# Who adds up the six modulation rows: a TensorE product per row, or VectorE and GpSimd sums with TensorE adding over partitions

## The chip, the cores and the metric

The kernel runs on one NeuronCore of a Trainium2 chip. The metric is the device time of one execution in microseconds (us). For the kernel before, three runs were timed: 2280.32, 2281.99 and 2283.0 us, median 2281.99. A hardware profile of one further execution lies beside them: that execution took 2280.29 us, and its span, from the first to the last instruction, is 2278.5 us. So 1.8 us lie outside the span, and the profiled execution stands at the lower end of the runs, 1.7 us under their median.

In what follows PE is the TensorE matmul unit and PEld its weight load, DVE is VectorE, ACT is ScalarE, POOL is GpSimd, and SP is the engine whose queue issues all DMAs here. An entry such as L244 is a line of the kernel.

## What is computed

A transformer block on 2048 tokens of width 576, in float32: 32 query heads of 18 channels share one key and value head, and the second half is an MLP of width 4608. Both halves are modulated. One vector `c` of 576 numbers goes through a silu and a 576 x 3456 matrix, and the result is cut into six rows of 576: shift, scale and gate for either half.

```
mod = (silu(c) @ w_mod).reshape(1, 6, 1, 576)
sa, ca, ga, sb, cb, gb = mod[:, 0], ..., mod[:, 5]
h = layernorm(x) * (1 + ca) + sa
x = x + ga * attention(h, wq, wk, wv, wo)
h = layernorm(x) * (1 + cb) + sb
x = x + gb * (gelu(layernorm(h) @ w1 + b1) @ w2 + b2)
```

Rows 0 and 1 are needed at once, before the first projection. Rows 3 and 4 (`sb`, `cb`), 2 (`ga`, folded into `wo`) and 5 (`gb`, folded into `w2` and `b2`) are needed later.

## The kernel before

The work on each engine stands in an order written out by hand; every engine runs its own instructions strictly in that order, and waits where an operand or a buffer is not ready. All DMAs share SP's queue, so an issue that waits holds up the ones behind it.

**Opening (about 0 to 33 us).** The first 512 tokens are loaded, normalised and transposed (`tr`, L152) into five PSUM tiles `hp`. Meanwhile rows 0 and 1 are made: for each row its five chunks of 128 rows of `w_mod` (`wm01`, tile `bigw`) are multiplied on PE with the silu of `c`, in two halves of 288 columns. `mod_mm` (L199) does that: `srep` holds each value of silu(c) 32 times over, so the five products of a half go to four strips of 32 partitions, and the strips hold partial sums. DVE copies them to `modr` (L201). `mod_cols` (L207) then turns a row into columns: a matmul with `sel`, a matrix with ones in partitions 0, 32, 64 and 96, adds the four strips. The result `mcol` is scale and bias of `h_evac` (L224), where ACT makes `hf` from `hp`, DVE casts it to the high half of `zt` (L226) and subtracts for the low half (L229). In between ACT and POOL split the projection weight `wqr` into `wqh` and `wql` (L379, L381), first the last 128 columns, then the first 504; DVE does the last 64 rows (L385).

**Projection (to 137 us).** The four token blocks `tb` are projected one after the other, five pieces (`q_chunk`, 14 matmuls of L244 each) a block. Of the first piece of a block, `k_block` (L287) makes keys as soon as the second piece has been issued; it reads the low half `qs[:,1]` that POOL made at L276. In the last block four `mod_bcast` steps are strewn between the pieces: rows 3 and 4 go through `mod_mm`, then `sel` as stationary matrix adds the strips and lays the sum on all 128 partitions at once (L217), and DVE stores it to `BC` (L218).

**Attention (137 to about 1402 us).** 32 quads of four heads. A quad takes 64 score matmuls (L855), each followed by an exponential on ACT (L857), the products with V (L845), and the row maxima of the next quad (L315 on PE, L877 on DVE). Scores and all odd jobs share the four PSUM buffers `psB`. The token strings `QUAD` and `QUADW` are that order. After each chunk `kc` of 16 the function `between` may advance two generators: `fill`, every second chunk, and `prep` (the MLP weights, on POOL), from quad 3 on. At the head of `fill` stands `late_weights`: rows 2 and 5 by `mod_bcast`, and then `wo` times row 2, on POOL (L511 to L513). In `between` a new query tile is cleared too (`new_q`, POOL, L132), which waits until PE is done with the quad three before. After a quad `post_quad` divides: DVE transposes and takes a reciprocal (L675, L678), POOL multiplies (L679), DVE transposes back (L681).

**MLP (to the end).** Nothing of the change lies there.

Of the kernel before, what the change touches and what calls it, by code (L numbers as in the profile page):

```python
# [18 lines left out]
KD = 5  # L19
# [13 lines left out]
def block_kernel(ctx: ExitStack, tc, x, wqkv, wo, w1, b1, w2, b2, c, wmod, ident_in, out):  # L33
# [52 lines left out]
    srep = pa.tile([128, KD, 32], F32, name="srep")  # L86
# [14 lines left out]
    for h2 in range(2):  # L101
        sy.dma_start(wm01[1][:, :, 288 * h2:288 * (h2 + 1)], wmod[1, :, :, 288 * h2:288 * (h2 + 1)])
# [9 lines left out]
    sel = pa.tile([128, 128], F32, name="sel")  # L112
# [3 lines left out]
    st = p1.tile([128, KD], F32, name="st")  # L116
# [74 lines left out]
    modr = p1.tile([128, 2, D], F32, name="modr")  # L191
    mcol = p1.tile([128, 2, KD], F32, name="mcol")

    def mod_mm(wm, h2, dst):

        pm = psB()
        for k in (0, 4, 1, 2, 3):
            g = 32 * (k % 4)
            pe.matmul(pm[g:g + 32, :288], srep[:, k, :], wm[:, k, 288 * h2:288 * (h2 + 1)],  # L199
                      start=(k < 4), stop=(k > 0))  # L200
        ve.tensor_copy(dst[:, 288 * h2:288 * (h2 + 1)], pm[:, :288])  # L201

    def mod_cols(j, pm):
        for m in range(KD):
            w = 128 if m < KD - 1 else 64
            for o in ((0,) if m < KD - 1 else (0, 64)):
                pe.matmul(pm[o:o + w, m:m + 1], modr[:, j, 128 * m:128 * m + w], sel[:, :1], start=True, stop=True)  # L207
        ve.tensor_scalar(mcol[:, j, :], pm[:, :KD], float(j), None, op0=ALU.add)

    def mod_bcast(wm, row, dst, add, scl):  # L210

        for h2 in range(2):
            mod_mm(wm, h2, row)
            yield
            cs = slice(288 * h2, 288 * (h2 + 1))
            p = psB()
            pe.matmul(p[:, :288], sel, row[:, cs], start=True, stop=True)  # L217
            ve.tensor_scalar(dst[:, cs], p[:, :288], scl, add, op0=ALU.mult, op1=ALU.add)  # L218
            yield

    def h_evac(p, zt, k, e, first=False):

        hf = p1.tile([128, TB], F32, name="hf", bufs=2)
# [153 lines left out]
    def split_wq(cs, es):  # L377
        for k in range(KD):
            ac.activation(wqh[:, k, cs], wqr[:, k, cs], AF.Copy)  # L379
        for k in range(KD - 1):  # L380
            es[k].tensor_tensor(wql[:, k, cs], wqr[:, k, cs], wqh[:, k, cs].bitcast(F32), op=ALU.subtract)  # L381
# [4 lines left out]

    pick = p1.tile([128, 2, 128], F32R, name="pick")
    ones = p1.tile([128, 1], F32, name="ones")
    ve.memset(pick.bitcast(F32), 0.0)
    for i, r in ((0, 0), (0, 2), (1, 1)):  # L390
        ve.tensor_copy(pick[:, i, :].rearrange("p (g c) -> p g c", g=2)[:, :, DH * r:DH * (r + 1)],
                       ident[:, None, 96:96 + DH].to_broadcast([128, 2, DH]))
    ve.tensor_reduce(ones, ident.rearrange("p (g c) -> p g c", g=2)[:, :, R3:], axis=AX.XY, op=ALU.add)
# [27 lines left out]
    split_rest(slice(0, 504))  # L421

# [17 lines left out]
    wm34 = []  # L440
    late = (x for j in range(2) for x in mod_bcast(wm34[j], modr[:, j], BC[:, j, :], float(j), 1.0))
    for tb in range(NB):
        nz = big() if tb + 1 < NB else None
        if tb >= 2:
            wm34.append(load_mod(tb + 1))
        for i, m in enumerate((4, 0, 1, 2, 3)):
# [14 lines left out]
            if tb == NB - 1:  # L461
# [4 lines left out]
                for _ in range((0, 1, 2, 2, 2)[i]):  # L466
# [883 lines left out]
```

## Time and profile before

| | |
|---|---|
| median of 3 runs | 2281.99 us |
| the profiled execution | 2280.29 us |
| its span | 2278.5 us |
| PE busy | 2241.0 us, 98% of the span |
| DVE busy | 1942.0 us, 85% |
| ACT busy | 1644.9 us, 72% |
| POOL busy | 1506.1 us, 66% |
| opening: first matmul for the keys of block 0 | at 33.31 us |
| first score matmul of quad 0 | at 137.00 us |
| quad 0, quad 1, quads 2 and 3 | 42.2, 41.0, 37.4 us each |

The quads are counted from the first exponential of one to the first of the next. A busy PE is not PE at its peak, since matmuls overlap and their ends are modelled; so a stage is read from when its pieces start, and from what a wait ended on, rather than from the busy shares.

### The profile page before, as it was taken

Reading aid. Unit: us, or ns where it says so; the run is one execution under the profiler, and the core shown is the slowest. Engines: PE = TensorE matmul, PEld = TensorE weight load, DVE = VectorE, ACT = ScalarE, POOL = GpSimd, SP = SyncE. Lnnn points to the kernel's source line nnn. Section 1 sums busy time; section 2 is a strip of 40 time slices with the busy share of each in tenths; the row PEclk is TensorE's granted clock in tenths of the full one; section 3 lists DMA queues with packets and bytes.
Section 4 is the critical chain, followed back from the end, with each engine's and each line's share of the span. In section 5 each row is a group of like instructions: output and inputs, shape, how many; then the busy total and the mean of one; then the engine's idle time right before and its main releaser. Section 6 shows DMA issues by size and latency. Waiting matters only on the chain.

```text
span 2278.5 us, 45948 instructions
## 1 busy us (share of the span) xinstructions
PE 2241.0 (98%) x16534; PEld 1446.2 (63%) x16534; DVE 1942.0 (85%) x3435; ACT 1644.9 (72%) x3141; POOL 1506.1 (66%) x1759
## 2 busy tenths in 40 slices
PE   8999999999999999999999999999999999999999
PEld 6644545444444444444444546888888878888888
DVE  6589999999999999999999974778888777787786
ACT  5558999999999999999999997444454444343443
POOL 6503366676787787677783002888888887767676
PEclk9999999999999999999999999999999999999999
DMA  6421234433433333333331002555656557666563
GB/s 225 138 99 49 73 124 142 136 128 117 135 124 121 119 132 114 119 125 123 119 129 64 20 7 83 180 174 178 177 173 180 160 151 215 180 178 179 177 181 117
DMA packets 184229, 305.58 MB, mean 134 GB/s; under 512 B 19275, under 2 KB 77515, under 8 KB 184001
## 3 DMA queue, kind: packets, MB, share of 16 engines
q1 hardware_dynamic: 184001, 302.64, 42.1%
q8 instruction: 131, 2.15, 0.4%
q14 instruction: 97, 0.79, 0.1%
HBM read 200.48 MB, written 93.19 MB: 129 GB/s over the span
## 4 chain that ended last, share of the span: by engine, by line
PE 90%; DVE 5%; POOL 2%; ACT 2%; issue 1%; DMA 0%; ACTq 0%; POOLq 0%; DVEq 0%
PE psC L845 22%; PE psB L1053 17%; PE psA L1150 16%; PE psB L855 14%; PE psM L315 11%; PE psB L657 2%; PE psB L244 2%; DVE mx L877 2%; PE psB L865 2%; PE psB L152 1%; ACT P L857 1%; PE psA L315 1%; PE psB L199 1%; PE psA L1180 1%; PE psA L657 1%
## 5 line engine op out<-in xcount | busy, mean ns | idle before, releaser
L857 ACT ACTIVATE P<-psB 128x512 f32<-128x512 f32 x2008 | 1044.8, 619 | 45.3 <-PE psM L315 18.4
L877 DVE TENSOR_REDUCE mx<-psM 128x1 f32<-128x512 f32 x1476 | 938.1, 683 | 42.4 <-PE psB L855 19.6
L315 PE MATMUL psM<-KS,qst 64*128 64x512 f32 x1722 | 600.1, 440 | 1.1 <-DVE mx L877 0.4
L855 PE MATMUL psB<-qst,KS 64*128 64x512 f32 x2008 | 584.5, 428 | 0.6 <-DVE mx L333 0.4
L845 PE MATMUL psC<-P,V 128*32 128x256 f32 (+3 forms) x6424 | 578.8, 448 | 0.5 <-ACT O L672 0.5
L855 PEld LDWEIGHTS psB<-qst,KS 64*128 64x128 f32 x2008 | 302.2, 184 | 215.6 <-ACT P L857 132.8
L1053 PE MATMUL psB<-ops,w1a 128*128 128x512 f32 x1512 | 395.7, 397 | 0.2 <-DVE h L1068 0.2
L315 PEld LDWEIGHTS psM<-KS,qst 64*128 64x128 f32 x1722 | 274.5, 184 | 157.2 <-DVE mx L877 122.4
L1053 PEld LDWEIGHTS psB<-ops,w1a 128*128 128x128 f32 x1512 | 271.4, 189 | 45.9 <-DVE h L1068 0.4
L1156 DVE TENSOR_TENSOR XT<-psA,XT 128x576 f32<-128x576 f32 x350 | 256.4, 753 | 18.5 <-PE psA L1150 11.5
L845 PEld LDWEIGHTS psC<-P,V 128*32 128x32 f32 x6424 | 139.4, 108 | 202.9 <-issue 176.7
L1150 PE MATMUL psA<-w2s,big 128*128 128x288 f32 x1680 | 248.3, 297 | 6.4 <-POOL big L1123 2.6
L1150 PEld LDWEIGHTS psA<-w2s,big 128*128 128x128 f32 x1680 | 240.0, 190 | 21.7 <-POOL big L1123 3.5
L1124 POOL TENSOR_TENSOR big<-s,big 128x512 fp32r<-128x512 f32 x140 | 181.9, 1299 | 11.2
L1066 ACT ACTIVATE psB<-gs 128x512 f32<-128x512 f32 x144 | 86.7, 602 | 135.5 <-DVE gs L1065 135.5
L1062 ACT ACTIVATE h<-psB,b1t 128x512 f32<-128x512 f32 x144 | 98.0, 680 | 109.1 <-PE psB L1053 93.7
L875 DVE CUSTOM_DVE_ANT_0 xc<-psM,xc 128x512 f32<-128x512 f32 x246 | 166.0, 681 | 3.7 <-PE psB L855 1.2
L868 ACT ACTIVATE xc<-psB 128x512 f32<-128x512 f32 x246 | 152.9, 622 | 11.9 <-PE psM L315 11.9
L691 POOL TENSOR_TENSOR os<-O,os 128x512 fp32r<-128x512 f32 x28 | 36.1, 1290 | 150.5 <-ACT os L690 150.5
L1065 DVE SCALAR_TENSOR_TENSOR gs<-psB,h 128x512 f32<-128x512 f32 x144 | 98.5, 684 | 39.3 <-ACT psB L1063 39.3
L718 POOL TENSOR_TENSOR r<-r,r 128x256 fp32r<-128x256 f32 (+1 forms) x162 | 121.4, 749 | 13.0
L132 POOL MEMSET qst<- 32x1024 f32 x62 | 58.6, 945 | 106.8 <-PE psB L855 69.0
(198 smaller groups left out, 3238.9 us busy)
## 6 DMA issues: line engine op xcount, KB each, us to landing
w1a<-w1scr SPq DMA_DIRECT2D x252, 256.0 KB
w2s<-w2sum SPq DMA_DIRECT2D x140, 288.0 KB
w1scr<-r SPq DMA_DIRECT2D x126, 256.0 KB
w2scr<-r SPq DMA_DIRECT2D x72, 288.0 KB
w2sum<-r SPq DMA_DIRECT2D x72, 288.0 KB
w2s<-w2scr SPq DMA_DIRECT2D x70, 288.0 KB
qst<-qscr SPq DMA_DIRECT2D x192, 72.0 KB
w1a<-w2scr SPq DMA_DIRECT2D x35, 288.0 KB
```

Source lines behind the costliest of these rows:

```text
L315: pe.matmul(o, QST[n][64 * g:64 * g + 64, p, 128 * qt:128 * (qt + 1)], KS[64 * g:64 * g + 64, 512 * kb:512 * (kb + 1)], start=True, stop=True)
L718: po.tensor_tensor(o[:, n:2 * n], src, o[:, :n].bitcast(F32), op=ALU.subtract)
L845: pe.matmul(PVt[n][32 * j:32 * (j + 1), cs], V[:, kc, :], t[:, j, cs], start=(kc == 0 and h0 == 0), stop=(kc == 15), skip_group_check=True)
L855: pe.matmul(t, KS[64 * g:64 * g + 64, 128 * kc:128 * (kc + 1)], QST[n][64 * g:64 * g + 64, i, :], start=True, stop=True)
L857: ac.activation(P[n, kc][:, 2 * i + g, :], t, AF.Exp, scale=SCALE)
L868: ac.activation(XC[-1], t, AF.Relu)
L875: ve.tensor_tensor_reduce(c, t, c, 1.0, -3.0e38, ALU.add, ALU.max, o)
L877: ve.tensor_reduce(o, t, axis=AX.X, op=ALU.max)
L1053: pe.matmul(o, x, y, start=(first and i == 0), stop=(i == len(terms) - 1), skip_group_check=True)
L1124: po.tensor_tensor(unit(u, 1), x, unit(u, 0).bitcast(F32), op=ALU.subtract)
L1150: pe.matmul(p[:, i, :288], x[:, ts_], W2S[k][:, y], start=(bool(first) and q == 0), stop=(q == 2), skip_group_check=True)
L1156: ve.tensor_tensor(o, p[:, :, :288], o, op=ALU.add)
```

## The change

- **Row 1** is no longer made by PE. Its load comes in three pieces by chunks (two, two, one) instead of two by columns. DVE multiplies chunk 0 with the per-partition value of silu(c) and adds the other four by `scalar_tensor_tensor` (`mod_sum`); every partition then holds a partial sum, and `mod_cols` adds over all 128 with a column of `unity`, a matrix of ones.
- **Row 0** stays on PE; of the fifth chunk each strip now takes 72 columns, 4 + 4 matmuls a half instead of 5.
- **The weight split** is given chunk by chunk; the last three chunks of 504 columns go behind `h_evac` on ACT, the last two on POOL. The low halves of `zt` of chunks 1 and 3 go from DVE to POOL, `hf` has three buffers instead of two, and `pick` and `ones` are made later.
- **Rows 2 to 5** are made in the first quads. All of 5, 2 and 3 are loaded when `fill` starts, 4 later. POOL multiplies each with silu(c) and adds the chunks in place (`scaled`, `added`: six instructions a row, 2880 elements a partition multiplied and 2304 added). `bcast` then needs two matmuls with `unity` for a row, one for each half, back to back, and two DVE stores. Nothing of it is left in the projection.
- `prep` begins in quad 4 instead of 3; in `ln2_rows` a step lies between loading and scaling `b2`; the buffer of the first attention output is taken in `late_weights`.

```
-    for h2 in range(2):
-        sy.dma_start(wm01[1][:, :, 288 * h2:288 * (h2 + 1)], wmod[1, :, :, 288 * h2:288 * (h2 + 1)])
+    for k0, k1 in ((0, 2), (2, 4), (4, 5)):
+        sy.dma_start(wm01[1][:, k0:k1], wmod[1, :, k0:k1])
...
-    def mod_mm(wm, h2, dst):
+    def mod_mm(h2):
         pm = psB()
-        for k in (0, 4, 1, 2, 3):
-            g = 32 * (k % 4)
-            pe.matmul(pm[g:g + 32, :288], srep[:, k, :], wm[:, k, 288 * h2:288 * (h2 + 1)],
-                      start=(k < 4), stop=(k > 0))
-        ve.tensor_copy(dst[:, 288 * h2:288 * (h2 + 1)], pm[:, :288])
+        c0 = 288 * h2
+        for k in range(KD - 1):
+            pe.matmul(pm[32 * k:32 * k + 32, :288], srep[:, k, :], wm01[0][:, k, c0:c0 + 288], start=True, stop=False,
+                      skip_group_check=True)
+        for k in range(KD - 1):
+            pe.matmul(pm[32 * k:32 * k + 32, 72 * k:72 * k + 72], srep[:, KD - 1, :],
+                      wm01[0][:, KD - 1, c0 + 72 * k:c0 + 72 * k + 72], start=False, stop=True, skip_group_check=True)
+        ve.tensor_copy(modr[:, 0, c0:c0 + 288], pm[:, :288])
+    def mod_sum(k):
+        row, w, c = modr[:, 1], wm01[1][:, k, :], st[:, k:k + 1]
+        if k:
+            ve.scalar_tensor_tensor(row, w, c, row, op0=ALU.mult, op1=ALU.add)
+        else:
+            ve.tensor_scalar(row, w, c, None, op0=ALU.mult)
...
-        hf = p1.tile([128, TB], F32, name="hf", bufs=2)
+        hf = p1.tile([128, TB], F32, name="hf", bufs=3)
...
-            mod_mm(wm01[0], t, modr[:, 0])
-    mod_mm(wm01[1], 0, modr[:, 1])
-    mod_cols(0, psB())
-    mod_mm(wm01[1], 1, modr[:, 1])
-    busy(2)
-    mod_cols(1, psB())
+            for k in (0, 1) if t == 0 else (2,):
+                mod_sum(k)
+            mod_mm(t)
+    for k in (3, 4):
+        mod_sum(k)
+    mod_cols(0, psB(), sel)
+    mod_cols(1, psB(), unity[:, :1])
     busy(5)
-    split_wq(slice(504, WQC), (po, po, po, po))
-    split_wq(slice(0, 504), (po, po, po, po))
     for k in range(KD):
-        h_evac(hp[k], zt, k, ve, True)
+        split_wq(k, slice(504, WQC))
+    for k in range(2):
+        split_wq(k, slice(0, 504))
+    for k in range(KD):
+        h_evac(hp[k], zt, k, po if k % 2 else ve, True)
         if k == 0:
             split_rest(slice(504, WQC))
+    for k in range(2, KD):
+        split_wq(k, slice(0, 504))
     split_rest(slice(0, 504))
...
-        if tb >= 2:
-            wm34.append(load_mod(tb + 1))
...
-                for _ in range((0, 1, 2, 2, 2)[i]):
-                    next(late)
...
     def late_weights():
...
+        def scaled(w, k0, k1):
+            po.tensor_tensor(w[:, k0:k1], w[:, k0:k1], st[:, k0:k1, None].to_broadcast([128, k1 - k0, D]), op=ALU.mult)
+        def added(w, k0, k1, n=1):
+            po.tensor_tensor(w[:, k0:k0 + n], w[:, k0:k0 + n], w[:, k1:k1 + n], op=ALU.add)
...
+        def bcast(w, dst, add, scl):
+            for h2 in range(2):
+                cs = slice(288 * h2, 288 * (h2 + 1))
+                p = psB()
+                pe.matmul(p[:, :288], unity, w[:, 0, cs], start=True, stop=True)
+                ve.tensor_scalar(dst[:, cs], p[:, :288], scl, add, op0=ALU.mult, op1=ALU.add)
+            yield
+        m3, m2, m5 = (bigw(D) for _ in range(3))
+        for j, t in ((5, m5), (2, m2), (3, m3)):
+            sy.dma_start(t, wmod[j])
...
+        for i in range(12):
+            for _ in range(2):
+                next(sums, None)
+            if i > 5 and i % 2:
+                next(rows)
+            yield
+        m4 = load_mod(4)
...
-        if n > 2 and kc not in quiet:
+        if n > 3 and kc not in quiet:
```

Three places show how instructions move. First PE in the last block of the projection, before, from the keys of the block (L287) to the first score matmul (L855); `bigw` is a modulation row, `modr` its partial sums, `mxf` the maxima of quad 0:

```order
L287 MATMUL psB<-qs,pick 128x512 x2
L293 MATMUL psB<-ident,qf 128x128 x4
L199 MATMUL psB<-bigw,srep 32x288 x5
L244 MATMUL psB<-big,wA 126x512 x7
L315 MATMUL psA<-KS,qst 128x512 x4
L244 MATMUL psB<-big,wA 126x512 x7
L217 MATMUL psB<-modr,sel 128x288
L199 MATMUL psB<-bigw,srep 32x288 x5
L244 MATMUL psB<-big,wA 126x512 x5
L315 MATMUL psA<-KS,qst 128x512 x4
L244 MATMUL psB<-big,wA 126x512 x5
```

And the same stretch after (L290 was L287, L247 was L244, L318 was L315):

```order
L290 MATMUL psB<-qs,pick 128x512 x2
L296 MATMUL psB<-ident,qf 128x128 x4
L247 MATMUL psB<-big,wA 126x512 x7
L318 MATMUL psA<-KS,qst 128x512 x4
L247 MATMUL psB<-big,wA 126x512 x12
L318 MATMUL psA<-KS,qst 128x512 x4
L247 MATMUL psB<-big,wA 126x512 x5
```

The `mod_mm` (L199) and `sel` (L217) steps are gone, here and twice more up to the first score matmul; the rest follows on unchanged.

Second, POOL in the opening after the change, from the first weight split (L383, before L381) to the low half of the first projected piece (L279, before L276):

```order
L383 TENSOR_TENSOR wA<-bigw,wA 128x128 x4
L383 TENSOR_TENSOR wA<-bigw,wA 128x504 x2
L232 TENSOR_TENSOR big<-hf,big 128x512 x2
L383 TENSOR_TENSOR wA<-bigw,wA 128x504 x2
L279 TENSOR_TENSOR qs<-qf,qs 128x512
```

Before, the eight splits stood together; now two subtractions for `zt`, which wait for DVE's casts, stand among them.

Third, DVE in the same stretch after the change, from the sums of row 1 (L215, L213) to the last chunk of `zt`; L207 stores halves of row 0, L222 the columns:

```order
L215 TENSOR_SCALAR modr<-bigw,st 128x576
L213 SCALAR_TENSOR_TENSOR modr<-bigw,st,modr 128x576
L207 COPY modr<-psB 128x288
L213 SCALAR_TENSOR_TENSOR modr<-bigw,st,modr 128x576
L207 COPY modr<-psB 128x288
L213 SCALAR_TENSOR_TENSOR modr<-bigw,st,modr 128x576 x2
L222 TENSOR_SCALAR mcol<-psB 128x5 x2
L229 CAST big<-hf 128x512
L232 TENSOR_TENSOR big<-hf,big 128x512
L387 TENSOR_TENSOR wA<-bigw,wA 64x128
L229 CAST big<-hf 128x512 x2
L232 TENSOR_TENSOR big<-hf,big 128x512
```

DVE gains the five sums, loses two copies, and of the five subtractions for `zt` (one behind each cast before) keeps those of chunks 0, 2 and 4.

More of the change, by code (lines that the diff above doesn't have):

```diff
@@ L111, in block_kernel @@
     ve.memset(nhalf, -0.5)
-    sel = pa.tile([128, 128], F32, name="sel")
+    unity = pa.tile([128, 128], F32, name="unity")
+    po.memset(unity, 1.0)
+    sel = p1.tile([128, 1], F32, name="sel")
+    srep = p1.tile([128, KD, 32], F32, name="srep")
     ve.memset(sel, 0.0)
@@ L385, in split_rest @@
         ve.tensor_tensor(o, wqr[64:, KD - 1, cs], o.bitcast(F32), op=ALU.subtract)
[L387 to L393, printed above, removed]
     def busy(n):
```

66 lines of the change are left out of this document (38 added, 28 removed).

## The prediction

> **What bounds the kernel now.** I read the page's totals and the chain first, then one row per stage, then the waits inside the stages that the change touches.
>
> ```profile
> span 2278.5 us, 45948 instructions
> ...
> PE 90%; DVE 5%; POOL 2%; ACT 2%; issue 1%; DMA 0%; ACTq 0%; POOLq 0%; DVEq 0%
> ```
>
> Nine tenths of the chain that ended last are PE. So the question for every edit is whether it takes a step out of PE's order, or a wait that PE sits in. The attention quads by stretches (columns: stretch, length, then busy time and count of PE, PEld, DVE, ACT, POOL, granted clock, DMA share, GB/s); each stretch runs from a quad's first exponential to the next one's:
>
> ```profile
> 137.60:179.80 42.20, 41.33 (x357) 20.07 (x356) 37.78 (x73) 36.63 (x73) 0.40 (x1) 0.96 0.23 81
> 179.80:220.80 41.00, 41.00 (x391) 19.87 (x393) 38.40 (x75) 37.51 (x77) 15.56 (x14) 1.00 0.17 54
> 220.80:258.20 37.40, 37.40 (x365) 18.50 (x364) 36.53 (x71) 36.96 (x77) 10.34 (x11) 1.00 0.07 21
> 258.20:295.60 37.40, 37.40 (x365) 18.52 (x365) 36.55 (x71) 37.01 (x77) 21.30 (x30) 1.00 0.35 111
> 295.60:332.90 37.30, 37.30 (x365) 18.47 (x361) 36.48 (x71) 36.89 (x76) 26.72 (x40) 1.00 0.43 142
> ```
>
> The reader is to see two things. A quad without modulation work takes 37.4 us with PE, ACT and DVE all near full, so an inserted step finds no room; quad 1, which has two halves of a row, takes 3.6 us more. And POOL's load does not matter there: 10.3, 21.3 and 26.7 us of it leave the quad at 37.4.
>
> **The change, part by part.** *Last projection block.* PE's order there, as its rows stand (PEld rows mark where a step's first weights go in):
>
> ```profile
> 111.55 1.16 PE L199 MATMUL psB<-bigw,srep 128*32 128x288 f32 x10 [0.34 <-ACT qs L275]
> 112.64 1.89 PE L244 MATMUL psB<-big,wA 128*126 128x512 f32 x7
> ...
> 116.62 0.42 PEld L217 LDWEIGHTS psB<-modr,sel 128*128 128x128 f32 x2
> 118.51 1.44 PE L244 MATMUL psB<-big,wA 128*126 128x512 f32 x5
> ...
> 124.05 0.42 PEld L217 LDWEIGHTS psB<-modr,sel 128*128 128x128 f32 x2
> 125.95 1.88 PE L244 MATMUL psB<-big,wA 128*126 128x512 f32 x7
> ...
> 130.69 0.22 DVE L346 TENSOR_REDUCE mxf<-mx 128x16 f32<-128x64 f32 x1
> 131.79 0.28 PE L353 MATMUL psB<-ident,mxf 128*16 128x128 f32 x1
> ```
>
> Three insertions go: 112.64 - 111.55 = 1.09, 118.51 - 116.62 = 1.89, 125.95 - 124.05 = 1.90, together 4.9 us. The two waits beside them (0.34 for ACT's read of a PSUM buffer) stay with the next piece. The fourth insertion ends at 131.79 with the transpose of the maxima of quad 0, which opens the way to the first score matmul; it also needs `mxf`, ready at 130.91, so there 131.79 - 130.91 = 0.9 less a semaphore, 0.8, is gained. Behind it DVE's reductions set the pace, as before. Sum 5.7. Ends: 4.9, if the last junction gives nothing, and 6.8, if `mxf` came early enough for the whole fourth step (1.9 like its neighbours). I take 5.7, since the row of `mxf` decides. The eight DVE stores and two 1.4 MB loads that leave this block lay beside other work: nothing.
>
> *Quads 0 and 1.* Quad 1's insertions, grouped over 179.8 to 220.8:
>
> ```profile
> L199 PE MATMUL psB<-bigw,srep 128*32 128x288 f32 x20 | 2.3, 413 | 0.0
> L217 PE MATMUL psB<-Z,sel 128*128 128x288 f32 x4 | 1.5, 458 | 0.0
> L679 POOL TENSOR_TENSOR T<-T,R 128x512 f32<-128x512 f32 x1 | 1.0, 1049 | 8.7 <-DVE R L678 8.7
> L511 POOL TENSOR_TENSOR bigw<-bigw,gab 128x576 f32<-128x576 f32 x4 | 5.7, 1427 | 0.0
> ```
>
> Two halves hold PE 2.3 + 1.5 = 3.8 us and cost 3.6: 0.95 of PE's time is lost. Before, four halves stand in quads 0 and 1: 4 x 1.8 = 7.2. After, eight products like L217 (0.75 each) stand in quads 1 and 2: 8 x 0.75 x 0.95 = 5.7. Gain 1.5. Ends: 0, if an insertion costs by its PSUM buffer and DVE store rather than by PE time (eight before and eight after), and 3.6, if the two back to back cost like one, 7.2 / 8 = 0.9. I take PE's time, because the two rows add up to the loss.
>
> What POOL must have done by then: per row 2880 elements multiplied by a broadcast, 2304 added. L511 gives 1427 / 576 = 2.48 ns an element; L679, with a broadcast operand, 1049 / 512 = 2.05. A row takes 11.6 to 12.8 us.
>
> ```profile
> 138.51 1.31 SPq L92 DMA_DIRECT2D bigw<-in_wmod  x2
> ...
> 189.62 0.24 DVE L678 RECIPROCAL R<-T 128x16 f32<-128x16 f32 x1
> ...
> 208.05 0.70 DVE L681 STREAM_TRANSPOSE O<-T 128x512 f32<-128x512 f32 x1
> ```
>
> The loads are issued where L92 stands, 5.7 earlier, at 132.8; 1.47 MB need 4.8 us at the opening's 310 GB/s (row below), so the first row can be summed from about 138.5, and the three are done by 151, 164 and 177. Quad 1 begins at 179.8 - 5.7 - 3.6 = 170.5; the three products stand at its chunks 1, 5 and 9, that is about 174, 184 and 195. Slack 18 us or more. Queued behind POOL's sums are the clearing of a query tile (wanted a quad later) and quad 0's division (L679): its R comes at about 180, DVE takes the result back at L681 some 18 us later. The fourth row has quad 2 to itself. So the POOL sums cost nothing; without that cover, the overshoot itself. `prep` one quad later:
>
> ```profile
> L718 POOL TENSOR_TENSOR r<-r,r x162: 723/736/817, 271.6 to 1216.5; 128x256 fp32r<-128x256 f32 x126, 128x288 fp32r<-128x288 f32 x36
> ```
>
> It would end near 1254 instead of 1217, far ahead of the MLP: nothing. The step in `ln2_rows` and the earlier `big` go with it.
>
> *Opening.* Here the sum is least sure.
>
> ```profile
> 0.00:20.00 20.00, 13.68 (x90) 9.75 (x91) 11.29 (x38) 6.85 (x15) 12.02 (x27) 1.00 0.93 310
> ```
>
> ```profile
> 16.99 4.00 ACT L379 ACTIVATE wA<-bigw 128x128 fp32r<-128x128 f32 x10 [2.65 <-DMA bigw<-in_wqkv]
> 17.38 6.57 POOL L381 TENSOR_TENSOR wA<-bigw,wA 128x128 fp32r<-128x128 f32 x8 [4.27 <-ACT wA L379]
> 22.38 0.17 DVE L208 TENSOR_SCALAR mcol<-psB 128x5 f32<-128x5 f32 x1 [1.14 <-PE psB L207]
> 22.58 1.45 ACT L224 ACTIVATE hf<-psA,mcol 128x512 f32<-128x512 f32 x2 [1.59 <-DVE mcol L208]
> 30.25 0.60 ACT L274 ACTIVATE qf<-psB 128x512 f32<-128x512 f32 x1 [1.82 <-PE psB L244]
> 31.42 1.30 POOL L276 TENSOR_TENSOR qs<-qf,qs 128x512 fp32r<-128x512 f32 x1 [7.47 <-ACT qs L275]
> 33.31 0.62 PE L287 MATMUL psB<-qs,pick 128*128 128x512 f32 x2
> ```
>
> Row 1's load is complete before 16.99, when the next transfer of the queue has landed. Five DVE sums, each some 0.75 (L1156 below, also 128x576), are done by about 18; one chain of six column products follows the other, and `mcol` is ready near 19.9 instead of 22.55: 2.6 us early. But then POOL is still at the splits, where before it had finished at 23.95 and left DVE alone with `zt`. What that does, the trace shows three times:
>
> ```profile
> L226 DVE CAST big<-hf x5: 420/422/851, 23.4 to 28.5; 128x512 fp32r<-128x512 f32 x5
> L229 DVE TENSOR_TENSOR big<-hf,big x8: 691/692/1250, 24.3 to 51.1; 128x512 fp32r<-128x512 f32 x8
> L1156 DVE TENSOR_TENSOR XT<-psA,XT 128x576 f32<-128x576 f32 x350 | 256.4, 753 | 18.5 <-PE psA L1150 11.5
> ```
>
> ```profile
> 1825.84 1.30 POOL L1124 TENSOR_TENSOR big<-s,big 128x512 fp32r<-128x512 f32 x1
> 1827.10 2.26 POOL L1074 TENSOR_TENSOR w1a<-h,gt 128x512 fp32r<-128x512 f32 x1
> 1825.93 2.29 DVE L976 TENSOR_TENSOR ops<-yr,ops 128x1024 fp32r<-128x1024 f32 x1
> ```
>
> The first cast, at 23.39, took 851 ns instead of 422: it ended 0.3 after POOL's last split. L229's 1250 fell on a POOL subtraction, and at 1825.9 the two took turns: DVE (2.29, shortest 1.18) waited for POOL's running instruction, POOL's next (2.26 for 1.30) for DVE. So a DVE cast or subtraction in SBUF and a POOL one do not overlap. [...]
>
> With turns taken: `hf` 20.0 to 20.8; cast 0 behind a split to 21.3; the second long split to 22.6; DVE's subtraction 0, the short rest and casts 1 and 2 to 24.2; POOL's subtraction 1 (1.29, like L276) to 25.5; DVE's 2 and casts 3 and 4 to 27.0; POOL's 3 to 28.3; DVE's 4 to 29.0, and the first piece ends near 29.3 (30.2 before). POOL then has two splits of 1.26, DVE's long rest (0.68) between them, and the 1.30 of L276: ready at about 33.3, where before it was at 32.7. The key product L287 waits for exactly that, and starts at 33.3 to 33.4 against 33.31. So what was won is waited for again: gain 0. Ends: -1.4, one more long POOL instruction in the way, and +3.3, nothing shared (then POOL's chain ends at 29.6 and L287 stands at 30.0).
>
> **Sum.** 0 + 5.7 + 1.5 = 7.2 us. Span 2278.5 - 7.2 = 2271.3, that execution 2273.1; it lies 1.7 under the median of the runs, so the median forecast is 2282.0 - 7.2 = 2274.8.
>
> **Rivals.** (a) *DVE and POOL hardly meet in the opening*, since the waits fall on gaps: 3.3 more, 2271.5. For it: POOL waits for DVE's casts anyway. Against: the three stretched rows. (b) With that, the products in the quads *cost by pairs* (3.6): 2282.0 - 5.7 - 3.3 - 3.6 = 2269.4. (c) *Insertions cost by count, and the opening loses 1.4*: 5.7 - 1.4 = 4.3, 2277.7. For it: each insertion takes a PSUM buffer from scores that ACT empties at full load. (d) *The last block hides what it loses*: if pieces wait for ACT or the maxima instead, half of 5.7 stays, and with 1.5 from the quads and a small loss in front about 3.5, 2278.5. Against: no gap of PE in those rows exceeds 0.34. (e) *Slower: PE waits for POOL's third row.* It decides from the point where 138.5 + 3 x row passes 195, 18.8 a row; the gain is gone at 21.2, 1.65 times the 12.8. At twice the rate, 25.6 a row, PE waits 20 us: 2295. For it: 2.26 instead of 1.30 at 1827.10. Against: DVE's reductions in the quads read PSUM, and L679 and L511 held their rate amid them.
>
> **How the numbers follow.** The forecast 0.50, (a) 0.17, (b) 0.05, (c) 0.14, (d) 0.05, (e) 0.06, another loss 0.03. A measurement here tells 0.2% (4.6 us) from no change. Faster: the forecast less 0.02 for its edge, (a) and (b): 0.70. Within: (c), (d) and the edge: 0.21. Slower: 0.09. The likeliest's own range is 2271 to 2278; the range of all, with (b) to (d) mostly in it, 2268.5 to 2280.
>
> **What would show it.** The first score matmul at about 131.3 instead of 137.0; the key product L287 still near 33.3, with POOL's `qs` row as its releaser and stretched casts before it; quads 0, 1 and 2 at about 38.6, 41.7 and 38.8 (three pairs of products in quad 1, one in quad 2); no wait of PE for POOL there; quads 3 on and the MLP as before. Wrong it is, if L287 stands at 30, if quad 1 is over 44, or if later quads change.

## The result, and the profile after

The changed kernel took 2273.34 us, the median of 6 runs (2272.95 to 2276.66); the kernel before, over 6 runs, 2280.28: the medians lie 6.9 us apart. The ratio, which is not the quotient of the two medians, is 0.9972 with a 95% interval of 0.996 to 0.9983, so 6.4 us less (3.9 to 9.1); a second set of runs gave 0.9968 (0.9956 to 0.998). Forecast were 7.2 us less and a median of 2274.8. The profiled execution has a span of 2271.4 us against a forecast of 2271.3. That the totals agree so closely is luck, as the stages of the two profiled executions show (us):

| stage | before | after | gained | forecast |
|---|---|---|---|---|
| up to the key product of the last block | 110.16 | 110.50 | -0.3 | 0 |
| from there to the transpose of the maxima | 21.63 | 16.30 | 5.3 | 5.7 |
| from there to the first score matmul | 5.21 | 6.54 | -1.3 | in the 5.7 |
| from there to the first exponential | 0.6 | 0.9 | -0.3 | 0 |
| quads 0 to 2 | 120.6 | 118.2 | 2.4 | 1.5 |
| quads 3 to 31 | 1137.9 | 1138.8 | -0.9 | 0 |
| MLP, not touched | 882.4 | 880.2 | 2.2 | 0 |

The 2.0 us that the last block fell short (forecast 5.7, 4.0 at the first score matmul, 3.7 at the first exponential) are made up by 2.2 us in a stage that the change does not touch. Each column is one execution. A second profile of the change gave, in the same order, 110.78, 16.28, 6.04, 0.9, 119.0, 1138.7 and 880.6.

The page of the changed kernel, the rows for its span and for the chain that ended last:

```profile
span 2271.4 us, 45796 instructions
...
PE 85%; DVE 4%; POOL 3%; ACT 2%; issue 1%; DMA 0%; SPq 0%; POOLq 0%; ACTq 0%
```

The chain is still PE's, with 85% against 90% before; no other engine has more than 4% of it. Now the opening, in rows of the timeline (start, busy time, engine and line, count, and in brackets the idle time before and what ended it):

```profile
18.76 0.16 DVE L222 TENSOR_SCALAR mcol<-psB 128x5 f32<-128x5 f32 x1 [1.08 <-PE psB L221]
...
20.42 1.65 DVE L232 TENSOR_TENSOR big<-hf,big 128x512 fp32r<-128x512 f32 x1
...
25.62 1.66 DVE L232 TENSOR_TENSOR big<-hf,big 128x512 fp32r<-128x512 f32 x1
27.31 1.63 DVE L387 TENSOR_TENSOR wA<-bigw,wA 64x504 fp32r<-64x504 f32 x1
26.68 3.39 POOL L383 TENSOR_TENSOR wA<-bigw,wA 128x504 fp32r<-128x504 f32 x2
30.04 1.31 POOL L279 TENSOR_TENSOR qs<-qf,qs 128x512 fp32r<-128x512 f32 x1
24.36 7.23 PE L247 MATMUL psB<-big,wA 128*128 128x512 f32 x24 [0.59 <-POOL big L232]
31.43 0.62 PE L290 MATMUL psB<-qs,pick 128*128 128x512 f32 x2
...
40.67 0.33 PE L154 MATMUL psB<-ident,Z 128*128 128x128 f32 x1 [0.92 <-DVE Z L191]
...
48.11 0.60 ACT L278 ACTIVATE qs<-psB 126x512 fp32r<-126x512 f32 x1 [1.33 <-DMA qscr<-qs]
48.76 1.88 PE L247 MATMUL psB<-big,wA 128*128 128x512 f32 x7 [1.80 <-ACT qs L278]
```

The piece of the last row, in the kernel before:

```profile
48.48 1.88 PE L244 MATMUL psB<-big,wA 128*128 128x512 f32 x7 [0.79 <-ACT qs L275]
```

`mcol` is ready at 18.92 (18.76 + 0.16) instead of 22.55. VectorE's subtractions (L232) take 1.65 where they took 0.69, because GpSimd works in SBUF at the same time. The key product (now L290) stands at 31.43, 1.9 us early. By the last three rows of the change and this one, that lead is waited for again inside the first two blocks: PE's wait at 48 us was 0.79 before and is 1.80 now, the wait of 0.92 for `Z` is new, and block 1's key product came at 56.79 before and at 57.05 after.

The junction between projection and quads, after, with the rows of SP's queue, POOL and DVE among it:

```profile
126.80 0.27 PE L356 MATMUL psB<-ident,mxf 128*16 128x128 f32 x1 [0.76 <-ACT qf L277]
...
129.05 0.49 PE L318 MATMUL psA<-KS,qst 64*128 64x512 f32 x1 [1.31 <-DVE mx L336]
...
131.33 2.07 PE L393 MATMUL psB<-ident 128*128 128x128 f32 x8
133.34 0.96 PE L899 MATMUL psB<-qst,KS 64*128 64x512 f32 x2
...
127.41 0.28 DVE L359 SCALAR_TENSOR_TENSOR ms<-psB,ms 16x128 fp32r<-16x128 f32 x1 [0.75 <-ACT ms L358]
127.36 1.27 POOL L279 TENSOR_TENSOR qs<-qf,qs 126x512 fp32r<-126x512 f32 x1 [2.82 <-issue]
124.57 4.39 SPq L283 DMA_DIRECT2D qscr<-qs  x2
129.47 2.84 SPq L363 DMA_DIRECT2D qst<-ms  x4
```

And the same place in the kernel before:

```profile
132.66 0.75 PE L217 MATMUL psB<-modr,sel 128*128 128x288 f32 x2
...
135.84 1.16 PE L399 MATMUL psB<-ident 128*128 128x128 f32 x8
132.40 0.28 DVE L356 SCALAR_TENSOR_TENSOR ms<-psB,ms 16x128 fp32r<-16x128 f32 x1
133.31 2.83 SPq L360 DMA_DIRECT2D qst<-ms  x4
```

Two things are to be seen. PE waits 0.76 and 1.31 where the row products stood, and the maxima `ms` leave for the query tile 1.8 us after they are made (127.69 to 129.47) instead of 0.6 (132.68 to 133.31): SP's queue has the store of the last query piece ahead of them, which waits for GpSimd's `qs` until 128.63. The store stood there in the kernel before too, but GpSimd's `qs` ended only 0.2 behind `ms` (at 132.87), where it now ends 0.9 behind. And the four short products at 131.33 take 2.07 instead of 1.16, because the granted clock, the share of its full speed that TensorE is allowed to run at, is halved. This view gives busy times and the granted clock (the 0.50 and 1.00 after the count of POOL) of the changed kernel by stretches:

```profile
20.60:27.40 6.80, 5.33 (x11) 3.35 (x12) 6.64 (x9) 3.57 (x6) 4.38 (x4) 0.50 1.02 375
...
126.40:129.80 3.40, 1.43 (x6) 0.57 (x6) 2.53 (x4) 0.97 (x3) 1.27 (x1) 1.00 0.27 96
129.80:140.10 10.30, 9.91 (x36) 6.36 (x40) 8.16 (x12) 5.85 (x12) 0.00 (x0) 0.50 0.61 206
```

In 126.4 to 129.8 PE was busy 1.43 of 3.40 us, and at half clock for the 10.3 us behind it. The kernel before had one such stretch of 3.4 us here (140.4 to 143.8) and none in the opening. That its row products had filled PE's waits is a guess at this point; the experiments come back to it. Last the quads 0 to 3:

```profile
134.20:172.60 38.40, 38.40 (x337) 19.32 (x338) 35.55 (x68) 36.55 (x74) 29.19 (x16) 0.92 0.35 126
172.60:213.80 41.20, 41.20 (x377) 20.31 (x373) 39.51 (x77) 37.34 (x77) 11.76 (x10) 1.00 0.28 90
213.80:252.40 38.60, 38.60 (x369) 19.17 (x365) 37.56 (x73) 36.99 (x76) 18.53 (x15) 1.00 0.08 21
252.40:289.80 37.40, 37.40 (x365) 18.41 (x369) 36.59 (x71) 36.97 (x76) 13.75 (x14) 1.00 0.08 22
```

They take 38.4, 41.2 and 38.6, where 38.6, 41.7 and 38.8 were forecast, with up to 29 us of GpSimd's sums in them and no wait of PE for POOL.

### The profile page after: what moved, and what is told of

It is laid out like the page before. It is cut to its first block, busy times and chain, and to the rows that moved or that the text cites. A ratio compares the mean times of both kernels' runs of the same rounds, so it can differ in the third digit from the quotient of the medians.

```text
span 2271.4 us, 45796 instructions
## 1 busy us (share of the span) xinstructions
PE 2230.7 (98%) x16442; PEld 1446.0 (64%) x16442; DVE 1945.6 (86%) x3428; ACT 1643.9 (72%) x3141; POOL 1554.2 (68%) x1786
## 4 chain that ended last, share of the span: by engine, by line
PE 85%; DVE 4%; POOL 3%; ACT 2%; issue 1%; DMA 0%; SPq 0%; POOLq 0%; ACTq 0%
PE psC L889 21%; PE psB L1097 17%; PE psA L1194 16%; PE psB L899 13%; PE psM L318 11%; PE psB L700 2%; DVE mx L921 2%; PE psB L909 2%; ACT P L901 1%; PE psA L1224 1%; PE psA L700 1%; PE psB L154 0%; PE psB L247 0%; DVE xc L919 0%; PE psB L356 0%
## 5 line engine op out<-in xcount | busy, mean ns | idle before, releaser
L901 ACT ACTIVATE P<-psB 128x512 f32<-128x512 f32 x2008 | 1044.8, 619 | 44.4 <-PE psM L318 16.5
L921 DVE TENSOR_REDUCE mx<-psM 128x1 f32<-128x512 f32 x1476 | 938.1, 683 | 42.2 <-PE psM L318 17.6
L318 PE MATMUL psM<-KS,qst 64*128 64x512 f32 x1722 | 602.4, 443 | 0.6
L318 PEld LDWEIGHTS psM<-KS,qst 64*128 64x128 f32 x1722 | 275.8, 185 | 156.0 <-DVE mx L921 119.2
L1109 DVE SCALAR_TENSOR_TENSOR gs<-psB,h 128x512 f32<-128x512 f32 x144 | 98.5, 684 | 39.7 <-ACT psB L1107 39.7
L1115 ACT ACTIVATE big<-h 128x512 fp32r<-128x512 f32 x36 | 22.8, 633 | 146.7 <-DVE h L1112 146.7
```

Of the source, the lines that this page charges most:

```text
L318: pe.matmul(o, QST[n][64 * g:64 * g + 64, p, 128 * qt:128 * (qt + 1)], KS[64 * g:64 * g + 64, 512 * kb:512 * (kb + 1)], start=True, stop=True)
L901: ac.activation(P[n, kc][:, 2 * i + g, :], t, AF.Exp, scale=SCALE)
L921: ve.tensor_reduce(o, t, axis=AX.X, op=ALU.max)
```

## The experiments

Ratios are to the kernel before on the same chip, with 95% intervals.

### The two halves of the change

Opening alone: the new opening, rows 2 to 5 as before. Late rows alone: the reverse.

Some lines of each, against the kernel before:

```
 opening alone:
-    mod_mm(wm01[1], 0, modr[:, 1])
...
+        mod_sum(k)
...
+        split_wq(k, slice(504, WQC))
...
+        h_evac(hp[k], zt, k, po if k % 2 else ve, True)
 late rows alone:
-            wm34.append(load_mod(tb + 1))
...
-                    next(late)
...
+            scaled(w, 0, 2)
...
+                pe.matmul(p[:, :288], unity, w[:, 0, cs], start=True, stop=True)
```

> The change's opening alone (row 1 summed on VectorE, weight split chunk by chunk, two subtractions of zt on GpSimd, pick and ones late); rows 2 to 5 as before. Theory of the prediction: the opening is worth 0, so the median stays within 2 us of the kernel before (2280); the first key product at about 31.4 as in the changed kernel, the key product of block 1 again at 57.0 or later against 56.8. Rival, the opening carries a part of the gain that the later stages merely keep: 2 to 3 us faster, about 2277.5, with the last block's pieces that much earlier. Rival, the pieces with half clock decide: the opening costs a microsecond or two, 2281 to 2282.

> The late rows alone (rows 2 to 5 summed by GpSimd in the quads, nothing of them in the projection, prep from quad 4); rows 0 and 1, weight split and opening as before. Theory of the prediction: all of the gain is here, about 7 us, 2273; first score matmul 5.7 ahead of the kernel before if the clock is full at the junction (131.3), 3.7 ahead (133.3) if it is halved there as in the changed kernel; quads 0 to 2 as 38.4, 41.2, 38.7. Rival, the opening carries part: 2275 to 2276. If it is faster than the whole change, under 2272, the new opening is a loss.

Opening alone: 2279.61 us against 2280.62 beside it, ratio 1.0001 (0.9992 to 1.001); key product of block 0 at 32.45, of block 1 at 57.63, of the last block at 111.08. Late rows alone: 2275.07, ratio 0.9977 (0.9968 to 0.9986), transpose of the maxima at 126.42, quads 0 to 2 of 39.7, 41.2 and 38.7. So the gain that can be measured, 5.2 us by the ratio, is the late rows', and the opening is worth nothing within about 2 us. What the whole change has beyond the late rows alone lies inside the intervals.

### Where the opening's lead is lost

```
     for k in (3, 4):
         mod_sum(k)
+    pick = p1.tile([128, 2, 128], F32R, name="pick")
+    ones = p1.tile([128, 1], F32, name="ones")
...
     mod_cols(0, psB(), sel)
...
-        qs = p1.tile([128, 2, TB], F32R, name="qs", bufs=2)
+        qs = p1.tile([128, 2, TB], F32R, name="qs", bufs=3)
```

> The changed kernel with one edit: pick and ones (four small VectorE steps and a reduction, 2.3 us there amid GpSimd's splits) are made before the column products, in VectorE's idle time at 17.3 to 18.8, instead of behind the long subtraction of the split. Theory: the 1.9 us that the first key product is earlier (31.4 against 33.3) are lost again in block 1 because pick delays the statistics of block 1 on VectorE by 1 us. Then the key product stands at 31.4 or a little earlier, block 1's key product at about 55.5 to 56.3 instead of 57.05, and the time falls by about 1 us to 2272. Rival: the loss has another cause (ScalarE's second read of a piece waiting on a DMA): block 1's key product stays at 57.0 and the time within 0.5 us. Rival: mcol is delayed by pick and the whole opening slides by 0.3 to 0.7 us.

> The changed kernel with pick and ones made early, as in the third run, and with three buffers instead of two for the query pieces qs in the projection. Theory: what the opening gains is lost again in the first block because ScalarE's qs of the last piece waits 1.33 us for the store of the piece two before, which stands on SP's queue behind six loads of a query tile; with a third buffer TensorE's wait of 1.80 (1.82 with pick early) at 48.2 to 48.8 falls to 0.3 or less, and the key product of block 1 comes at about 55.0 instead of 56.5, the whole time 1 to 2 us less than with pick early alone. Rival: the next thing in line (statistics or the store itself) is as late, and block 1's key product stays at 56 or later.

The last two lines are the second kernel's alone. With `pick` early alone, 2273.96 (0.9971, 0.9961 to 0.998): PE's wait for `Z` falls from 0.92 to 0.26, the wait at 48 us stays at 1.82, and block 1's key product comes at 56.53, 0.5 earlier. With the third buffer too, 2273.47 (0.9968, 0.9956 to 0.998), and in the timeline of that kernel the wait is gone:

```profile
47.60 1.88 PE L247 MATMUL psB<-big,wA 128*128 128x512 f32 x7 [0.36 <-ACT qs L278]
```

Block 1's key product stands at 55.90 and the maxima are transposed at 125.59, 1.2 us ahead of the change. Block 0 began late that time (key product at 32.86), which shortens the wait by itself: two kernels with the change's own order here (those of GpSimd's slack below), with the key product at 33.1 and 32.9, wait 0.81 and 0.65. The kernel with all pieces together, at the end of the experiments, settles it: block 0's key product at 31.60, the same wait 0.36, block 1's at 55.10, both 1.7 ahead of the kernel before. So the two causes together account for the lost lead. What each is worth alone is not shown: in six executions with the change's own order, block 1's key product lay between 56.27 and 58.00, and `pick` early alone, 56.53, lies among them. The medians cannot tell so little.

### Do VectorE and GpSimd take turns?

```
-        h_evac(hp[k], zt, k, po if k % 2 else ve, True)
+        h_evac(hp[k], zt, k, ve, True)
```

> The changed kernel with the low halves of zt of chunks 1 and 3 back on VectorE, so that GpSimd has only the weight splits and qs. Theory of taking turns (the two engines do not overlap on SBUF work): VectorE has 2 x 0.69 more, GpSimd 2 x 1.3 less; GpSimd's chain to qs is 1.3 to 2.6 us shorter, the key product at about 30 instead of 31.4, the time 0 to 1 us less if block 1 keeps it. Rival, each engine runs by itself: VectorE's chain gets 1.4 us longer, the last piece of zt later by that, and the key product at 31.4 or 32.5.

2273.94 us (0.9973, 0.9963 to 0.9982), and the key product at 32.84, later and not earlier, near the 32.5 of the rival. That time alone decides nothing (six executions with the change's own opening had it between 31.43 and 33.10); the rows do:

```profile
23.31 0.69 DVE L232 TENSOR_TENSOR big<-hf,big 128x512 fp32r<-128x512 f32 x1
...
26.05 1.50 DVE L229 CAST big<-hf 128x512 fp32r<-128x512 f32 x1
27.58 1.62 DVE L232 TENSOR_TENSOR big<-hf,big 128x512 fp32r<-128x512 f32 x1
25.49 3.17 POOL L383 TENSOR_TENSOR wA<-bigw,wA 128x504 fp32r<-128x504 f32 x2 [3.54 <-ACT wA L381]
29.26 3.74 PE L247 MATMUL psB<-big,wA 128*128 128x512 f32 x15 [1.16 <-DVE big L232]
```

While GpSimd had nothing to do (21.95 to 25.49) a subtraction took 0.69. GpSimd's two splits then came 1.2 us sooner, and the last cast and subtraction beside them took 1.50 and 1.62 instead of 0.42 and 0.69, and PE waits 1.16 for that subtraction. So the two do hold each other up; the expected gain fell, since the splits slid forward in front of the last chunk. The 1.62 is 0.69 and 0.93 more, most of one long split of GpSimd (1.27 at the most in the kernel before).

### The half clock

In the opening seven short products were added, at the junction nine; nothing reads them.

```
 opening:  busy(7) for busy(5); 3 and 2 products of ident inside the first piece
 junction: busy(2); smax_fin2(0); unit(); busy(5); unit(2); busy(4)
```

> The changed kernel with seven more short TensorE products of the identity (results unused) where TensorE waits in the opening: two behind the column products, three and two inside the first piece, at its waits of 0.88 and 0.59 us. Theory: the granted clock is 0.50 from 20.6 to 27.4 because TensorE does little in the stretch before (24 column products of one column each, and waits), where the kernel before has no such stretch; with more work it stays at 1.00, the first piece ends up to 1 us sooner, the key product is at 30.4 to 31.0 instead of 31.4, and the time falls by 0 to 1 us. Rival: VectorE's and GpSimd's turns set the pace, and the clock is hidden behind them: the key product stays at 31.4 or comes 0.3 later. If the stretch of half clock stays, the theory on its cause falls.

> The changed kernel with nine more short products of the identity (results unused) in the waits between the projection and the quads: two ahead of the transpose of the maxima (wait 0.76), five and two at the waits of 1.31 and 0.64 for VectorE's maxima. Theory: of the 5.7 us forecast for the last block 2.0 are missing because TensorE is idle for half of the stretch 126.4 to 129.8 and the granted clock falls to 0.50 from 129.8 to 140.1; with the waits filled, the clock stays at 1.00 until at least 137, the first score matmul comes at 132.2 to 132.6 instead of 133.3, quad 0 takes 1 us less, the last exponential is 1.5 to 2.5 us sooner and the time 2271 to 2272. Rival: the fillings delay the maxima by as much, first score matmul at 133.3 or later, time unchanged or 1 us more. Rival: the clock falls all the same.

Opening filled: no half clock there any more, yet the key product at 31.39, just as without, and 2274.25 us (0.9964, 0.9952 to 0.9977). So the rival has the price: the turns of VectorE and GpSimd set the pace. Where half clock lasted 10 us in the opening (three runs), the key product came at 32.9 to 33.1, so that much is not hidden.

Junction filled: 2270.78 (0.9953, 0.994 to 0.9967), the lowest median but one of all; its five runs (2268.98 to 2274.79) still overlap with those of the two neighbours on its chip that leave the junction as it is (2272.24 to 2275.64). Its windows, and its first score matmul:

```profile
127.80:131.20 3.40, 3.40 (x22) 2.34 (x22) 2.64 (x3) 0.45 (x2) 1.27 (x1) 1.00 0.28 93
131.20:141.00 9.80, 8.40 (x50) 4.30 (x54) 8.38 (x12) 6.58 (x13) 0.00 (x0) 1.00 0.59 190
```

```profile
133.70 0.47 PE L903 MATMUL psB<-qst,KS 64*128 64x512 f32 x1 [0.82 <-DMA qst<-ms]
```

The clock stays full, and quad 0 takes 37.6 instead of 38.4, next to the 37.4 of a quad without extra work. From the transpose to the first score matmul it is 6.03 us instead of 6.54, and what ends the wait is now the transfer of `ms`. All twelve profiles with the new late rows bear the 0.5 out: where half clock set in within 3.5 us of the transpose (seven of them) that distance is 6.50 to 6.54, where it set in later or not at all (five) 5.87 to 6.28; the kernel before has 5.21. That the store ahead of `ms` on SP is the cause of the rest is read from the rows; another order was not tried. Of the 2.4 us by which this span is shorter than the change's, 1.5 lie in the MLP (878.7 against 880.2), and these are no work of the fillings, as will be seen. (In absolute time the score matmul is late, since this execution's block 1 began at 58.00.)

One profile a kernel says little of a throttle that differs from execution to execution. So here is the half clock of all fourteen profiles at the two places:

| | opening | junction |
|---|---|---|
| row products in place | none, none | 3.4 us, 3.4 us |
| taken out | 3.4 to 10.2 us in ten of ten | 6.8 or 10.2 us in ten of ten |
| taken out, waits filled | none, 3.4 us | none, 6.8 us |

The granted clock that each run's result lists (its mean over the run) goes the same way. Two sets of runs of the change have 0.992 to 0.995, mean 0.9935; 67 runs of the kernel before average 0.9955; junction filled has 0.995 to 0.997, and all pieces together, below, 0.995 to 0.998. So taking the products out lowers the clock, and filling the waits brings it back, though not in every execution. The price: among the 67 runs, those at 0.994 took 2282.9 us on average (13 runs), those at 0.997 2279.1 (18). A stretch of 3.4 us at 0.50 takes 0.00075 from the mean, which makes it some 0.9 us a stretch, an estimate from these runs.

In the MLP, which no kernel but the one with all pieces together touches, a stretch goes with more. Stretches of 3.4 us at half clock in it (without one in the last 1.5 us of every profile), and its time:

| stretches | MLP, us | kernels |
|---|---|---|
| 4 | 882.4, 882.4, 882.8, 882.9 | before, opening alone, pick early, subtractions back |
| 3 | 880.0 to 881.7 | the change (twice: 880.2, 880.6), late rows alone, GpSimd x 1.5, opening filled, qs with three buffers, all together |
| 2 | 878.7, 878.8, 878.9 | junction filled, products apart, GpSimd x 2 |

About 2 us a stretch, and kernels with the very same MLP lie in all three rows; among those that share the change's late rows there are 2, 3 and 4. So the 2.2 us "gained" there need no cause in the change: it is one stretch fewer. Whether the change makes such a stretch less likely is not shown, since both kernels without its late rows have four.

### How much slack have GpSimd's sums?

```
             scaled(w, 0, 2)
+            again(w, 0, 2)       # w times ones, same size; twice in the second kernel
```

> The changed kernel with GpSimd's sums made longer: each of the three multiplications of a row is followed by one of the same size with ones, so a row takes 16.2 us instead of 10.9; the values stay the same. Theory: the sums are hidden. They start at 143.1, the third row would be done at 191.6, and its product stands at 197.9: no wait, time within 1 us of the changed kernel. Rival: GpSimd's load costs as such (VectorE's division waits for its part of it, or the two slow each other): quads 0 to 2 longer, 2 us or more.

> The changed kernel with GpSimd's sums twice as long: each multiplication of a row is followed by two of the same size with ones, 21.4 us a row; the values stay the same. Theory, the slack worked out in the prediction: TensorE waits for the third row. Done at 143.1 + 3 x 21.4 = 207.3 against its product at 197.9: a wait of 9.5 us on GpSimd, and some more where VectorE waits for GpSimd's part of quad 0's division, which is queued behind the sums; the time is 9 to 14 us longer, 2283 to 2288, slower than the kernel before. Rival, the buffers and the order absorb it: under 3 us.

With one more multiplication a row took 16.5 us: 2272.8 (0.9958, 0.9944 to 0.9972), quads 1 and 2 of 41.2 and 38.7, no wait. With two more it took 22.0: 2287.79 (1.0027, 1.0018 to 1.0037), slower than before, and in its timeline:

```profile
207.39 2.29 PE L532 MATMUL psB<-bigw,unity 128*128 128x288 f32 x4 [10.22 <-POOL bigw L506]
```

A wait of 10.2 us where 9.5 was worked out. That the third row was done at 207.3, just as reckoned, is in part luck: its rows took longer than the 21.4 assumed, and the sums began at 141.2 and not at 143.1. The profiled execution is the fastest of ten (2282.86), and 10 us above the profile of the other kernel; the medians of the two lie 15 us apart. With half clock from 200.7 to 211.0, in the wait and behind it, quad 1 is 11.8 us longer than in the change; what the further 5 us of the median are is open. Here load on GpSimd cost nothing as long as it was done before PE read its result (16.5 us a row), and beyond that at least all of it (22.0).

### Pairs or singles

```
                 ve.tensor_scalar(dst[:, cs], p[:, :288], scl, add, op0=ALU.mult, op1=ALU.add)
-            yield
+                yield
...
-            if i > 5 and i % 2:
+            if i > 5:
                 next(rows)
```

> The changed kernel with the two products of a late row no longer back to back: a step of fill lies between them, so eight single insertions stand in quads 1 and 2 (six and two) instead of four pairs. Theory of the prediction: an insertion costs by its TensorE time, so nothing changes: quads 1 and 2 stay at 41.2 and 38.7. Rival, an insertion costs by its PSUM buffer and VectorE store whatever its size, and a pair costs once (1.27 us measured a pair): six times 1.27 in quad 1 is 45.0, quad 2 39.9, 5 us slower in all. In between: 1 to 2 us.

2273.68 us (0.9973, 0.9963 to 0.9984). One single product fell into quad 0, five into quad 1 (not six), two into quad 2; the windows of quads 1 and 2:

```profile
173.50:214.90 41.40, 41.40 (x377) 19.70 (x379) 39.03 (x76) 37.57 (x77) 10.61 (x9) 1.00 0.28 89
214.90:253.90 39.00, 39.00 (x369) 18.99 (x368) 37.53 (x73) 37.24 (x76) 15.24 (x13) 1.00 0.08 21
```

A single costs (41.4 - 37.4) / 5 = 0.80, a pair (41.2 - 37.4) / 3 = 1.27, so 0.63 a product; forecast was 0.71. An insertion costs about its time on PE, and standing in pairs saves 0.17 a product. The cost by count (1.27 a single) is out.

### All together, and the change once more

The pieces of the runs above that paid, and seven short products at the MLP's start:

```
+        if v == 1:
+            p = psA()
+            for _ in range(7):
+                pe.matmul(p[:, 0, :128], ident, ident, start=True, stop=True)
```

> The changed kernel with the three things that the other runs speak for, and one more of the same kind: pick early and three buffers for qs (0.6 and 0.6 us at the last block's end); short products of the identity in the waits of the opening and of the junction; and seven such products at the start of the MLP, where TensorE waits 2.22 and 0.82 us for GpSimd at 1423.7 to 1427.2 and the granted clock halves for one or two stretches of 3.4 us behind it. Theory, that these stretches are what the wait costs on top of itself: no stretch of half clock before 1800, first score matmul 1 to 1.5 us ahead of the changed kernel's, quad 0 some 1 to 2 us shorter, MLP 878.7 as in the run with the filled junction, in all 3 to 6 us under the changed kernel, 2267 to 2270. Rival: the gains fall on waits that take their place: 2271 to 2273.

> The changed kernel as it is, beside the run before it on one chip, for the difference between the two and for one more profile of it. Theory: median 2272.5 to 2274.5, quads 0 to 2 as before within 0.5 us but for the stretches of half clock, whose number (two or three in the opening, two or three at the junction, one or two at the MLP's start) differs between executions of one and the same program and moves a profile by 1 to 2 us a stretch. Rival: the stretches lie where they lay, and the difference between the MLP of the two kernels, 2.2 us, is the change's own.

Together: 2270.4 us (0.9952, 0.9939 to 0.9964); the change beside it 2274.51 (0.9968, 0.9956 to 0.998). The medians differ by 4.1 us and the five runs (2269.75 to 2272.98) lie almost wholly below the six (2272.67 to 2275.55), though the intervals of the ratios overlap. It is no better than the filled junction alone, lies between the forecast (2267 to 2270) and the rival (2271 to 2273), and its theory held in part only. (The profiled execution is the slowest of the five, 2272.98, at a mean clock of 0.995; the others had 0.997 or 0.998.) The first score matmul came at 130.80, 2.3 us ahead of the change's 133.10. But stretches of half clock came all the same, at 20.6, 133.2 and 1426.9: at the last two PE had been busy 68% and 56% of the 3.4 us ahead, with waits that the fillings left (0.83 for `ms`; 0.66 and 0.82 for GpSimd). Quad 0 took 39.6 and the MLP 881.7.

The change itself came out with the same quads 1 and 2 (41.2 and 38.7), and quad 0 at 39.1: this time half clock reached to 141.3. Its MLP had three stretches again and took 880.6, so for these two kernels the rival is not refuted by this run; what speaks against it is the table above.

## Why the prediction was right, point by point

- **Opening, 0.** Right in the sum (alone 1.0001, and -0.3 at the last block), right that VectorE and GpSimd take turns (1.65 for 0.69), wrong on the place. The key product was to stay at 33.3 and came at 31.4: `mcol` was ready 1.0 us earlier than reckoned (18.9, not 19.9), GpSimd's second subtraction ended 7.8 behind it instead of 8.4, and the splits and `qs` took 4.6 behind that instead of 5.0. The loss fell on two waits that the sum did not have: `Z` of block 1 behind `pick` on VectorE, and a store of `qs` behind query loads on SP's queue.
- **Last block, 5.7.** The term was too large by 1.7 to 2.0. "Behind it DVE's reductions set the pace, as before" is the step that failed. Up to the transpose 5.3 of the 5.7 were gained; behind it 1.3 was lost. Of it 0.8 stays when the clock is full, and there the transfer of the maxima ends the wait; it is issued 1.78 after `ms` instead of 0.63. The other 0.5 is the half clock. The removed product at 132.66 had stood in a wait of PE (0.63 before, 1.31 now) and gave nothing. The sign that the prediction named, the first score matmul at about 131.3, did not come: it stood at 133.34.
- **Quads, 1.5.** Measured 2.4. The price by PE's time was right (0.63 to 0.80 a product against 0.71). Forecast quad 0, 42.2 - 3.6 = 38.6, agrees with 38.4 by chance: at full clock it is 37.6, and each kernel has a loss of its own in it. Before it is 1.0 (42.2 - 3.6 - 37.6), most of it two waits of PE for VectorE's maxima at its start (0.41 and 0.36, ahead of the half clock at 140.4); after it is 0.8 for half clock.
- **POOL's sums, hidden.** Right, with 10.9 us a row against 11.6 to 12.8; they began at 143.1, not 138.5, because the loads were issued at 134.7, not 132.8, behind the transfers of the junction on SP, and the first sum could begin 8.4 us after that, not 5.7. From 143.1 + 3 x row = 197.9 the point where they cost is 18.3 a row (forecast 18.8): 16.5 was free and 22.0 was not.
- **`prep` a quad later, nothing; later quads as before.** Quads 3 to 10 are as before within 0.1. But quads 3 to 31 took 1138.6 to 1139.4 in all twelve profiles with the new late rows, against 1137.9 and 1138.1 in the two without: 0.9 in the change, 0.5 of it in quad 11 (41.3 to 41.7 against 40.8 and 41.1). "If later quads change" was one of the prediction's signs of being wrong, and by this much they did. The cause is open; `prep`, which now runs a quad later, was not tried by itself.
- **The MLP, as before.** Its 2.2 us go with one stretch of half clock fewer, and are no part of what was forecast. Without them the profile's gain is 4.9 us; the late rows alone gave 5.2 over the runs.
- **The rivals.** (a), VectorE and GpSimd hardly meet, is out: three subtractions of 1.65. (b) falls with it. (c), cost by count, is out by the products apart. (d), the last block hides what it loses, is true for a third: 3.7 of 5.7 reached the first score matmul. (e) is real at twice the work, with a wait of 10.2, and far off at the work there is.

## What to carry to other kernels

Work that TensorE did in its own waits cost nothing here (the product removed at 132.66 gave nothing) and helped to keep its clock up (3.4 us of half clock at the junction with the row products, 6.8 or 10.2 without): whoever takes such work out should look at what is left in the 3.4 us around it, and at a few spare products in the wait (with them none in one profile, 6.8 us in the other). GpSimd's sums were free up to the slack at the place where the result is read (each of three rows was done 22 us before its product, so 7.4 a row, since they queue behind one another; 16.5 us a row instead of 10.9 brought no wait), and beyond it PE waited for all of the rest (10.2 us at 22.0 a row). A stage time of a single execution that moves by a stretch or two of half clock, here 2 to 4 us in the MLP, says nothing of an edit. A step ahead of a chain over a DMA gains only what the queue lets through (`ms` left 1.78 us after it was made instead of 0.63): look for what stands ahead on SP and what that waits for.

## What the hardware showed that was not expected

TensorE's granted clock fell to 0.50 in steps of 3.41 us (before, one from 140.40 to 143.81; after, two from 20.59 to 27.42 and three from 129.82 to 140.06), behind a stretch of that length in which PE had been partly idle (busy 74, 85 and 42% of it). At the junction PE had been busy 39 to 74% of it, with no gap over 1.31, and the half clock then lasted one to three such stretches, though PE was busy 87 to 100% in them. Being partly idle is not enough, however: in the MLP of the change's own profile PE was busy 49% of 1843.25 to 1846.66, with a wait of 1.8, and 58% of 2249.50 to 2252.91, and the clock stayed full behind both. Which work counts is open. In quad 0 up to 3.4 us of half clock cost nothing (37.6 in four kernels with 1.6 to 3.4 us of it, as with none), and 5.9 us cost 0.8 (38.4 in the change).
